# Contractions over 448 rows as pairs of 64-row passes, with the loads and the start rearranged

## Chip, cores, metric

One core of one Trainium2 chip. The metric is the device time of one execution in microseconds (us). Most executions agree within 0.3%. A ratio of two kernels is the mean of one kernel's fast runs over the mean of the other's fast runs of the same rounds on the same chip, so it is not quite the ratio of the medians quoted beside it. The profile's "span" runs from the first to the last instruction; timed runs lie about 2 us above it.

## The reference, cut to what matters

```python
# S = 2048 tokens, D = 448, 16 query heads, 8 KV heads, Dh = 256, window W = 512, F = 1792
xn = layernorm(x)
q  = xn @ wq                                 # 448 -> 4096
p  = softmax(q k^T / 16)                     # over the last 512 keys
s  = (p v) @ wo                              # 4096 -> 448
g  = silu((gelu(xn @ w_gate) * (xn @ w_up)) @ w_down)
out = x + s * g
```

Two stages contract over D = 448: gate/up and Q. A full TensorE pass here contracts over 128 rows, and 448 = 3 x 128 + 64 = 7 x 64.

## The kernel before

A small planner records operations in program order, and puts each on one engine with semaphore waits. Order within an engine is program order, so what is emitted first is issued first. Matmuls write to PSUM, eight banks of 512 columns; a bank is free again when ScalarE or VectorE has read it out (evacuation). The tokens are 4 chunks of 512. Gate/up is 56 units (4 chunks of 14 blocks of 128 columns), and each unit makes a gate and an up tile of 128 x 512. Three 128-row passes and one 64-row remainder make a tile. Remainders of gate (rows 0 to 63) and up (rows 64 to 127) run side by side:

```python
def gu_full(n, b, first, halves=1):          # cut: halves
    for (w, bl, bb) in ((wg, b_wgl[wi], b), (wu, b_wul[wi], b + 1)):
        mms([(bank[bb], w[:, k, cols], xnT[:, k, toks], first and k == 0, (not first) and k == 2, False)
             for k in range(3)], ...)
def gu_rem(n, b, first):
    mms([(bank[b],     wg[0:64, 3, cols],   xnT[0:64, 3, toks],   first, not first, False),
         (bank[b + 1], wu[64:128, 3, cols], xnT[64:128, 3, toks], first, not first, False)], ...)

for sg in range(NSG):                        # a superunit is four units
    n = 4 * sg
    gu_full(n, 0, True); gu_full(n + 1, 2, True)
    ln_more()                                # statistics, normalization, DMA transpose of one more token tile
    gu_rem(n, 0, False);  gu_evac(n, 0)      # evacuation: Gelu on ScalarE, product on VectorE
    gu_rem(n + 1, 2, False); gu_evac(n + 1, 2)
    gu_rem(n + 2, 4, True); gu_rem(n + 3, 6, True)
    gu_full(n + 2, 4, False); gu_evac(n + 2, 4)
    ln_more()
    gu_full(n + 3, 6, False); gu_evac(n + 3, 6)
    if sg == 1:
        for i in range(Hq // 4): load_wq(i)  # 12 DMAs, issued by GpSimd
        for g in range(Hkv): load_v(g)       # 8 more
    if sg == 6: ...                          # K, wo, residual x
    if sg in {5: 0, 8: 1, 11: 2}: down(...)
```

The normalization needs 1/sqrt(var), and that is made by two tiny GpSimd operations:

```python
def ln_stats(t):                             # cut
    K.op("dve",  ... bn_stats, bn_aggr ...)
    K.op("pool", ... ve = var + eps ...)
    K.op("pool", ... rstd = ve ** -0.5 ...)
```

Q is built four heads at a time in the same form. Then for each head: scores (8 matmuls of 512 columns), Exp on ScalarE, value product (16 matmuls of 257 columns), and VectorE divides. `wo` follows once per chunk (128 matmuls of 448 columns).

The softmax here doesn't subtract the row's maximum and nothing guards it: scores larger than these inputs give would overflow.

## Time and profile before

585.99 us median of 3 (585.34 to 586.48), span 583.7 us.

The profile page of the kernel before: the busy tenths of TensorE and its granted clock in 40 equal slices (14.6 us each), and the chain of waits by engine.

```profile
PE   3939999999999999999999999999999999999997
...
PEclk9978999999999999999999999999999999999999
...
PE 92%; POOL 3%; DMA 2%; DVE 1%; ACT 1%; issue 0%; SPq 0%; DVEq 0%
```

TensorE is the limit nearly everywhere. The third slice (29 to 44 us) has a hole, and the clock is below full in the third and fourth slices.

"Busy" hides what a pass costs, because passes overlap: one of 512 columns is recorded as 379 ns long. What tells is the distance between starts (a slot: one pass, or one pair of 64-row passes): 216 ns for 512 columns, 189.5 for 448, 113 for 257, and 216.5 for a pair of 64-row passes (whose two starts are 3 to 4 ns apart). Times their counts:

| stage | slots | ns | us |
|---|---|---|---|
| gate/up | 392 | 216.5 | 84.9 |
| Q | 448 | 216.5 | 97.0 |
| scores | 512 | 216 | 110.6 |
| value product | 1024 | 112.7 | 115.4 |
| wo | 512 | 189.5 | 97.0 |
| down | 224 | 189.5 | 42.4 |
| sum | | | 547.3 |

So 36.4 us of the span are not this work. The largest piece is the hole. The timeline of TensorE in the kernel before (start in us, length, engine, line, operation; in brackets the idle time before it and what ended it):

```profile
31.55 0.81 PE L308 MATMUL bank<-xnT,wg 128*128 128x512 bf16 x3
42.09 1.46 PE L308 MATMUL bank<-xnT,wu 128*128 128x512 bf16 x3 [9.74 <-DVE actT L445]
43.35 1.49 PE L308 MATMUL bank<-xnT,wg 128*128 128x512 bf16 x3
44.63 1.49 PE L308 MATMUL bank<-xnT,wu 128*128 128x512 bf16 x3
```

The timeline of GpSimd in the same stretch:

```profile
26.27 0.57 POOL L353 TENSOR_TENSOR rstd<-ve,nhalf 128x1 f32<-128x1 f32 x1
26.78 7.33 POOL L293 DMA_DIRECT2D wq<-in_A_wq_dram  x12
34.10 5.97 POOL L293 DMA_DIRECT2D va<-in_A_v_cache_dram  x8
40.09 0.24 POOL L351 TENSOR_SCALAR ve<-mv 128x1 f32<-128x1 f32 x1
```

And of VectorE:

```profile
28.52 0.18 DVE L350 BATCH_NORM_AGGREGATE mv<-stats 128x2 f32<-128x6 f32 x1
41.02 0.41 DVE L358 TENSOR_SCALAR xn<-x_65,mv,rstd 128x512 bf16<-128x512 bf16 x1 [12.32 <-POOL rstd L353]
```

Read the three together: GpSimd issues loads for 13.3 us, the small rstd operation stands behind them, VectorE stands behind rstd, the products that would free PSUM stand behind the normalization, and TensorE runs out of PSUM banks. After the hole three 512-column passes take 1.28 us from start to start instead of 0.65: the clock is granted at half until 47.5 us.

The second piece is spread out. The timeline of TensorE, one mixed group of the kernel before:

```profile
140.36 0.81 PE L308 MATMUL bank<-xnT,wu 128*128 128x512 bf16 x3
141.10 0.39 PE L308 MATMUL bank<-xnT,wg 64*128 64x512 bf16 x1
141.11 0.39 PE L308 MATMUL bank<-xnT,wu 64*128 64x512 bf16 x1
141.33 0.38 PE L308 MATMUL bank<-xnT,wg 64*128 64x512 bf16 x1
...
141.76 0.38 PE L308 MATMUL bank<-xnT,wg 64*128 64x512 bf16 x1
141.77 0.38 PE L308 MATMUL bank<-xnT,wu 64*128 64x512 bf16 x1
142.07 0.82 PE L308 MATMUL bank<-xnT,wg 128*128 128x512 bf16 x3
```

From 141.76 to 142.07 is 0.31 us where 0.216 would do, and it is the same on the way in (140.36 to 141.10 is two steps of 0.216 and one of 0.31). A change costs 95 ns, and there are sixty. The Trainium skill, "TensorEngine Tiling (Array Packing)", Key Properties, says that changing the tiling mode drains TensorE. This trace fits that, and gives the price.

Third, where the last down block meets the first scores:

```profile
161.74 1.92 PE L308 MATMUL bank<-qT,kT 128*128 128x512 bf16 x7
164.66 1.95 PE L308 MATMUL bank<-qT,kT 128*128 128x512 bf16 x8 [1.00 <-ACT expT L299]
```

### The profile page before, as it was taken

How to read it: one execution, taken by the hardware profiler on the slowest of the kernel's cores; microseconds unless marked ns; L12 is line 12 of the kernel's file. 1: busy time of each engine (PE TensorE's matmuls, PEld its weight loads, DVE VectorE, ACT ScalarE, POOL GpSimd, SP SyncE). 2: the span in 40 equal slices, each digit the busy share in tenths (PEclk: the TensorE clock that was granted, in tenths of full speed). 3: DMA queues.
4: the chain of work that ended last, by engine and by line, in shares of the span. 5: the costliest groups of instructions: out<-in, count | busy, mean ns of one | idle time of the engine just before them, and what ended most of it. 6: DMA issues, size and time to landing. Idle time of an engine off the chain costs nothing.

```text
span 583.7 us, 8116 instructions
## 1 busy us (share of the span) xinstructions
PE 559.8 (96%) x3260; PEld 300.8 (52%) x3260; DVE 274.3 (47%) x729; ACT 205.1 (35%) x270; POOL 43.1 (7%) x85
## 2 busy tenths in 40 slices
PE   3939999999999999999999999999999999999997
PEld 2313444444455565555565555556556456556653
DVE  3616543434345665513565561265566217557532
ACT  2313232323264455402446441135543203553500
POOL 5382220000000000000000000100000000000000
PEclk9978999999999999999999999999999999999999
DMA  9997599000003311311322230132232113243221
GB/s 255 253 312 168 126 166 161 5 0 2 1 18 55 73 38 36 73 33 31 73 47 46 55 68 21 45 66 43 41 73 47 35 40 53 44 65 60 42 45 33
DMA packets 96565, 41.53 MB, mean 71 GB/s; under 512 B 87840, under 2 KB 92848, under 8 KB 96528
## 3 DMA queue, kind: packets, MB, share of 16 engines
q1 hardware_dynamic: 90864, 24.17, 23.4%
q0 software_dynamic: 4416, 15.70, 10.0%
q10 hardware_dynamic: 1248, 1.15, 0.6%
q8 instruction: 26, 0.43, 0.3%
q14 instruction: 11, 0.09, 0.1%
HBM read 18.71 MB, written 1.84 MB: 35 GB/s over the span
## 4 chain that ended last, share of the span: by engine, by line
PE 92%; POOL 3%; DMA 2%; DVE 1%; ACT 1%; issue 0%; SPq 0%; DVEq 0%
PE bank L308 92%; DMA wu<-in_B_w_up_dram 1%; POOL wq L293 1%; POOL va L293 1%; DMA x_65<-in_A_x_dram 1%; DVE actT L445 0%; POOL rstd L353 0%; DVE stats L349 0%; ACT L299 0%; ACT gl L299 0%; ACT expT L299 0%; POOL wg L293 0%; POOL ve L351 0%; SPq L293 0%; DVE xn L358 0%
## 5 line engine op out<-in xcount | busy, mean ns | idle before, releaser
L299 ACT ACTIVATE expT<-bank 128x1024 bf16<-128x1024 f32 x128 | 124.0, 1021 | 145.9 <-PE bank L308 145.9
L546 DVE TENSOR_SCALAR onorm<-bank,rden 128x256 bf16<-128x256 f32 x256 | 123.8, 484 | 9.3 <-DVE rden L544 0.3
L308 PE MATMUL bank<-va,expT 128*128 128x257 bf16 x1024 | 123.4, 273 | 0.0
L308 PE MATMUL bank<-qT,kT 128*128 128x512 bf16 x512 | 121.1, 379 | 1.1 <-ACT expT L299 1.0
L308 PEld LDWEIGHTS bank<-va,expT 128*128 128x128 bf16 x1024 | 98.4, 98 | 27.2 <-DVE onorm L546 3.0
L308 PE MATMUL bank<-xnT,wq 128*128 128x512 bf16 (+1 forms) x512 | 105.1, 379 | 0.0
L308 PE MATMUL bank<-wo,oT 128*128 128x448 bf16 x512 | 97.5, 352 | 0.0
L308 PEld LDWEIGHTS bank<-qT,kT 128*128 128x128 bf16 x512 | 49.7, 98 | 55.3 <-ACT expT L299 1.9
L522 DVE CAST qT<-bank 128x512 bf16<-128x512 f32 x64 | 42.8, 689 | 68.7 <-PE bank L308 68.7
L308 PEld LDWEIGHTS bank<-wo,oT 128*128 128x128 bf16 x512 | 50.1, 98 | 46.8
L308 PE MATMUL bank<-xnT,wu 128*128 128x512 bf16 (+2 forms) x230 | 61.8, 386 | 10.0 <-DVE actT L445 9.7
L308 PEld LDWEIGHTS bank<-xnT,wq 128*128 128x128 bf16 (+1 forms) x512 | 41.2, 97 | 55.8 <-issue 13.6
L299 ACT ACTIVATE qT<-bank 128x512 bf16<-128x512 f32 x64 | 36.6, 598 | 91.0 <-PE bank L308 91.0
L544 DVE RECIPROCAL rden<-bank 128x1 f32<-128x1 f32 x256 | 40.9, 160 | 58.0 <-PE bank L308 58.0
L308 PE MATMUL bank<-xnT,wg 128*128 128x512 bf16 (+2 forms) x230 | 61.6, 385 | 0.0
L299 ACT ACTIVATE gl<-bank 128x512 bf16<-128x512 f32 x56 | 31.9, 596 | 67.0 <-PE bank L308 67.0
L445 DVE TENSOR_TENSOR actT<-bank,gl 128x512 bf16<-128x512 f32 x56 | 36.9, 687 | 27.7 <-ACT gl L299 21.9
L566 DVE SCALAR_TENSOR_TENSOR tmp<-bank,g_57 128x448 f32<-128x448 f32 x16 | 10.0, 624 | 77.8 <-PE bank L308 77.8
L308 PE MATMUL bank<-wd,actT 128*128 128x448 bf16 x224 | 43.0, 352 | 0.0
L293 POOL DMA_DIRECT2D xr<-in_A_x_dram x16 | 8.6, 540 | 396.4 <-DVE ofin L569 396.4
L308 PEld LDWEIGHTS bank<-xnT,wu 128*128 128x128 bf16 (+1 forms) x230 | 21.7, 100 | 30.6 <-DVE actT L445 10.2
L308 PEld LDWEIGHTS bank<-xnT,wg 128*128 128x128 bf16 (+1 forms) x230 | 20.6, 100 | 32.4 <-issue 13.4
(28 smaller groups left out, 114.8 us busy)
## 6 DMA issues: line engine op xcount, KB each, us to landing
wo<-in_A_wo_dram POOLq DMA_DIRECT2D x4, 896.0 KB, 10.3
wq<-in_A_wq_dram POOLq DMA_DIRECT2D x4, 768.0 KB, 8.1
va<-in_A_v_cache_dram POOLq DMA_DIRECT2D x8, 256.0 KB, 11.8
oT<-onorm SPq DMA_TRANSPOSE x128, 2.5
xr<-in_A_x_dram POOLq DMA_DIRECT2D x16, 112.0 KB, 2.3
out_dram<-ofin SPq DMA_DIRECT2D x16, 112.0 KB, 1.7
wd<-in_B_w_down_dram POOLq DMA_DIRECT2D x1, 1568.0 KB, 12.4
wq<-in_A_wq_dram POOLq DMA_DIRECT2D x8, 128.0 KB, 8.0
```

The lines of the kernel that those rows point to most:

```text
L293: K.op(q, lambda e, o=o, i=i: e.dma_start(o, i), reads, writes, dma=True)
L299: K.op("act", lambda e, o=o, i=i: e.activation(o, i, func, scale=scale), reads, writes)
L308: ins = e.matmul(o, lhsT=l, rhs=r, start=st, stop=sp)
L445: K.op("dve", lambda e: e.tensor_tensor(actT[:, c % 2, f, :], bank[b + 1], gl[:, s, :], ALU.mult), (b_ps[b + 1], b_gl[s]), (b_actT[c % 2][ ...
L522: K.op("dve", lambda e: e.tensor_copy(qT[:, i, h4, 1, :], bank[b + 1]), (b_ps[b + 1],), (b_qT[i][h4][1],))
L544: K.op("dve", lambda e, bb=bb, r=r: e.reciprocal(rden[:, r:r + 1], bank[bb][:, Dh:Dh + 1]), (b_ps[bb],), (b_rden[r],))
L546: K.op("dve", lambda e, bb=bb, r=r, t4=t4: e.tensor_scalar(onorm[:, o, t4, h % 2, :], bank[bb][:, 0:Dh], rden[:, r:r + 1], None, op0=ALU.m ...
L566: K.op("dve", lambda e: e.scalar_tensor_tensor(out=tmp[:, s, :], in0=bank[b][:, 0:D], scalar=0.5, in1=g2[:, t, :], op0=ALU.mult, op1=ALU.m ...
```

## The change

Every contraction over D becomes seven 64-row pairs and nothing else. Weights of one output sit in partitions 0 to 63, those of another in 64 to 127, and the transposed activations are held twice, once in each half. Gate pairs with up. In Q a head pairs with the head four further on, so Q is built for 8 heads at a time. In the same change the loads, the start, the Exp table, the order around the last down block and the tail are rearranged. The core of the diff (cuts marked):

```diff
-        xnT [P, 4, S]; wg, wu [P, 4, F]; wq [P, 4, HD]
+        xnT [P, NK, S]; wgu [P, NK, F]; wq [P, NK, NG, HG // 2, 2, P]     # NK = 7, HG = 8, NG = 2
+        def pair(b, w, x, ks, start, stop, lo=0, hi=QC):
+            return [(bank[b + j][:, lo:hi], w(k)[R * j:R * j + R], x(k)[R * j:R * j + R],
+                     start and k == ks[0], stop and k == ks[-1]) for k in ks for j in range(2)]
   ... normalization writes 7 x 2 x 64 columns, each 64 twice, in place of 512:
+            src = x4[:, t, :].rearrange("p (k r) -> p k r", r=R).unsqueeze(2).broadcast_to([P, NK, 2, R])
   ... loads: the second copies of x's last 64 columns are gone; gate/up weights on the SP queue
   ... (the first up block on ScalarE's), w_down behind x and ahead of every transpose:
+        load_x("sp", 8, 8)
+        dma("sp", wd[:, :, :], B_w_down.rearrange("(f p) d -> p f d", p=P), (), (b_wd,))
   ... start: warm-up matmuls on zeros, half-units (units for 256 of their 512 tokens)
   ... between the transposes of tiles 2 and 3:
+        warm(14, 3)
+        ln_stats(0); ln_stats(1); ln_norm(0); ln_tp_pe(0, ...); warm(2, 3)
+        ln_norm(1); ln_tp_pe(1, [("dve", 4, 0, 4), ("act", 5, 4, NK)]); warm(3, 3)
+        ln_stats(2); ln_stats(3); gu(0, 0)
+        ln_norm(2); ln_tp_pe(2, ...); gu(1, 0); ln_norm(3); ln_tp_pe(3, ...); gu(2, 0)
   ... units: statistics of a tile in an even unit, its normalization in the odd unit after
+        for n in range(NQC * NF):
+            gu(n); gu_evac(n); ...
-            if sg == 1:                     # wq, V
+            if n == 27:                     # wq, V, K: behind the last rstd (unit 24)
+        DOWN_AT = {NF + 1: 0, 2 * NF + 3: 1, 3 * NF + 1: 2}
+        act(tmp[:, 1, 0:1], nhalf[:, :], ACT.Exp, ...)          # loads Exp's table ahead of Q
   ... first scores before the last down block; last output tile in two halves of 224 columns
```

## The prediction

> **What bounds it now.** TensorE. The chain of waits is 92% matmuls; the page gives PE 96% busy. Reading the distance between matmul starts in the timeline: a 512-column pass starts every 216 ns, a 257-column one every 113 ns, a 448-column one every 189.5 ns, and a pair of 64-row passes (starts 4 ns apart) every 216.5 ns. Multiplied by their counts (gate/up 392 slots, Q 448, scores 512, value 1024, output 512, down 224) this is about 547 us that the PE cannot avoid. Span 583.7 less 547 leaves 37 us:
> - start: first gate matmul at 11.3 us, then about 1 us at half clock and a 0.4 us wait for weights;
> - one hole at 32.2 to 42.1 us (9.9 us). Timeline: GpSimd issues 12 wq and 8 va loads from 26.8 to 40.1 us, and the tiny ops that make rstd stand behind them; VectorE, in order, waits 12.3 us for rstd, so it does not drain PSUM. The clock record shows half clock to 47.5 us, which costs another 2.7 us;
> - about 60 changes between 128-row and 64-row passes: the start distance is 308 to 312 ns there instead of 216, so 94 ns each, 5.7 us. The Trainium skill, "TensorEngine Tiling (Array Packing)", Key Properties, says that changing the tiling mode drains TensorE; this trace agrees and prices it;
> - 1.6 us at 163 us, where the first Exp waits for Tanh and a 1.28 us table load;
> - 3.9 us after the last matmul start.
>
> **What the change does.** The number of PE slots does not fall: two outputs cost 6 full passes plus one pair before, 7 pairs after, 7 slots either way. More weight loads (14 for 8), but the two halves load together in about 95 ns, inside the 216 ns slot. So the pairing itself gains only changes of mode: gate/up keeps them only around the three down blocks, Q has 8 groups in place of 16 pair blocks, about 22 left. Gain 3.5 us.
>
> The larger gain is in what moves with it. wq, va go to unit 27, after the last rstd (unit 25): the 9.9 us hole and its 2.7 us of half clock go. Exp's table is loaded before Q, and the first scores come before the last down block: 1.6 us go. The last output block is halved: 0.5 us.
>
> Start: the duplicate x loads go (the first norm waits 2.1 us for them before), and warm-up matmuls precede. But normalization writes 896 columns instead of 512 (0.41 us before; 0.65 to 1.0, estimated by size), each tile has 7 transposes instead of 4, and tiles 2 and 3 come late: I estimate the first half-units at 8.5 us and gap-free running from 13.6 us, 2.3 us of work being done by then.
>
> xnT's DMA transposes get 7/4 as long and queue behind wd (6 us to landing before); tile 7 is needed at about 34 us, I expect it by 30. VectorE in chunk 0 carries at most 2.5 us per 3.0 us.
>
> **Sum.** 13.6 + (547.3 - 2.3) + 2.1 changes of mode + 3.4 tail = 564 us span; the timed runs lie 2 us above: 566 us, range 560 to 573. Over 2% faster: 0.95; within: 0.04; slower: 0.01.
>
> **Right if:** no PE wait above 1 us after 15 us; pairs in Q and gate/up stay at 216 to 217 ns; the 308 ns steps fall to about 22; clock full from about 15 us; DVE waits for rstd under 2 us.
>
> **Wrong if:** long rows of pairs run slower than four do (10 ns per slot is 8 us); the weights, now to 64 partitions per transfer, land after 10 us; a longer start cools the clock; xnT transposes arrive late at chunk 1; the broadcast norm is much over 1 us.

## The result, and the profile after

566.75 us median of 4 (565.94 to 567.22) against 586.23; ratio 0.9669 (95% interval 0.9652 to 0.9686). It is 3.3% faster. Span 565.4 us.

The page of the changed kernel, the same lines (slices of 14.1 us):

```profile
PE   7989999999999999999999999999999999999997
...
PEclk9999999999999999999999999999999999999999
...
PE 93%; DVE 3%; issue 1%; DMA 1%; POOL 1%; ACT 0%; DVEq 0%; ACTq 0%
```

The large hole and the half clock are gone. A small hole is left, in the third slice. From the waits view, who waited for rstd in the kernel before (in all, times, longest, us):

```profile
DVE xn L358 <- POOL rstd L353: 26.0, 13, 12.3
```

and in the changed kernel:

```profile
DVE xn L356 <- POOL rstd L350: 5.8, 15, 0.5
```

The timeline of TensorE in the changed kernel, one Q group of 8 heads between a value product and the next scores:

```profile
179.79 2.23 PE L308 MATMUL bank<-va,expT 128*128 128x257 bf16 x18
181.95 12.26 PE L308 MATMUL bank<-xnT,wq 64*128 64x512 bf16 x112
194.37 2.97 PE L308 MATMUL bank<-qT,kT 128*128 128x512 bf16 x13 [0.16 <-issue]
```

In this long row of pairs the two starts lie 3 to 4 ns apart and the next pair follows 216 ns after the last, as in the short rows of before. Going in, the step is 207 ns after a 257-column pass instead of 113, and the next is 227 instead of 216. Coming out, the records are 535 ns apart, because the record of the first score pass is missing in this profile (15 of the 16 are there, 13 of them in this window). In profiles of the later variants x_best and a_no_warm, whose Q stage is the same, it is there: 308 ns after the last start, and the next follows 227 ns later. So a change costs about 106 ns in these long rows too, each way. After the start there are 21 changes in place of 60: six around the three down blocks, seven into Q (the first Q group follows gate/up directly) and eight out of it.

The start of the changed kernel, from the timeline of TensorE:

```profile
8.96 1.06 PE L308 MATMUL bank<-xnT,wgu 64*128 64x256 bf16 x14 [0.29 <-DVE mv L347]
10.72 0.56 PE L372 MATMUL bank<-ident,xn 128*128 128x128 bf16 x7 [0.70 <-DVE xn L356]
11.21 0.94 PE L308 MATMUL bank<-xnT,wgu 64*128 64x256 bf16 x14
12.28 0.56 PE L372 MATMUL bank<-ident,xn 128*128 128x128 bf16 x7
12.78 1.48 PE L308 MATMUL bank<-xnT,wgu 64*128 64x256 bf16 x24
```

From 12.78 us it runs without a gap, with two half-units (1.5 us) already done. The hole that is left, same view:

```profile
29.66 2.97 PE L308 MATMUL bank<-xnT,wgu 64*128 64x512 bf16 x26
34.71 3.20 PE L308 MATMUL bank<-xnT,wgu 64*128 64x512 bf16 x28 [2.09 <-DMA xnT<-xn]
```

and the SP queue ahead of it (here length is the time over which the group is issued):

```profile
10.78 5.20 SPq L296 DMA_DIRECT2D wd<-in_B_w_down_dram  x1
20.03 17.02 SPq L299 DMA_TRANSPOSE xnT<-xn  x6
```

Unit 14 is the first of chunk 1 and needs tiles 4 to 7. The semaphore records say: w_down lands at 30.7 us, the transpose issued at 20.03 (tile 4) at 31.5, that of tile 7, issued at 31.2, at 34.6.

What stands around the 547.3 us of passes, term by term. Each is read from the distances between starts, the clock record and the ends of the span:

| us | before | after |
|---|---|---|
| first gate matmul, less work done by gap-free running | 11.3 | 12.8 - 1.5 = 11.3 |
| half clock and weights at the start | 1.5 | 0 |
| hole near 32 us | 9.9 | 2.25 |
| half clock after it | 2.7 | 0 |
| changes of mode | 60 x 0.106 = 6.4 | 21 x 0.106 = 2.2 |
| scores around the last down block (wait for its product on VectorE, then for Exp) | 1.4 | 0.3 |
| from the last matmul's start | 4.2 | 3.2 |
| sum with 547.3 | 584.7 (span 583.7) | 566.6 (span 565.4) |

Most of what the sums lie above the spans is the 0.8 us by which 547.3 is high. The count of slots is the same in both columns: 448 rows cost 7 slots for two outputs, either as 6 full passes and one pair, or as 7 pairs.

### The profile page after: what moved, and what is told of

Same layout as the page of the kernel before. It is cut to its first block, busy times and chain, and to the rows that moved or that the text cites. A ratio compares the mean times of both kernels' runs of the same rounds, so it can differ in the third digit from the quotient of the medians.

```text
span 565.4 us, 9758 instructions
## 1 busy us (share of the span) xinstructions
PE 553.6 (98%) x4037; PEld 310.6 (55%) x4073; DVE 284.3 (50%) x736; ACT 209.3 (37%) x272; POOL 34.5 (6%) x70
## 4 chain that ended last, share of the span: by engine, by line
PE 93%; DVE 3%; issue 1%; DMA 1%; POOL 1%; ACT 0%; DVEq 0%; ACTq 0%
PE bank L308 93%; DVE actT L426 1%; DVE stats L346 1%; POOL rstd L350 1%; DVE xn L356 1%; DMA xnT<-xn 1%; DMA x_65<-in_A_x_dram 0%; PE bank L372 0%; POOL ve L348 0%; DVE mv L347 0%; DVE xnT L382 0%; DVE g_57 L437 0%; ACT gl L302 0%; ACT tmp L302 0%; PE bank L390 0%
## 5 line engine op out<-in xcount | busy, mean ns | idle before, releaser
L308 PE MATMUL bank<-qT,kT 128*128 128x512 bf16 x476 | 115.9, 379 | 2.9 <-issue 1.3
L308 PE MATMUL bank<-xnT,wq 64*128 64x512 bf16 x896 | 98.1, 376 | 0.0
L308 PE MATMUL bank<-wo,oT 128*128 128x448 bf16 (+1 forms) x544 | 97.6, 341 | 0.0
L308 PE MATMUL bank<-xnT,wgu 64*128 64x512 bf16 (+1 forms) x826 | 86.0, 366 | 2.4 <-DMA xnT<-xn 2.1
L308 PEld LDWEIGHTS bank<-wo,oT 128*128 128x128 bf16 x544 | 53.1, 98 | 44.0
L308 PEld LDWEIGHTS bank<-xnT,wq 64*128 64x128 bf16 x896 | 43.0, 94 | 52.9 <-issue 1.5
L308 PEld LDWEIGHTS bank<-xnT,wgu 64*128 64x128 bf16 x826 | 39.8, 94 | 47.9 <-DVE actT L426 2.6
L563 DVE SCALAR_TENSOR_TENSOR tmp<-bank,g_57 128x448 f32<-128x448 f32 (+1 forms) x17 | 10.2, 597 | 82.5 <-PE bank L308 82.5
L308 PEld LDWEIGHTS bank<-wd,actT 128*128 128x128 bf16 x224 | 21.7, 98 | 21.2 <-issue 1.3
L437 DVE SCALAR_TENSOR_TENSOR g_57<-tmp,bank 128x448 bf16<-128x448 f32 x16 | 9.9, 622 | 33.8 <-ACT tmp L302 33.8
## 6 DMA issues: line engine op xcount, KB each, us to landing
wgu<-in_B_w_gate_dram SPq DMA_DIRECT2D x2, 560.0 KB, 11.5
```

Of the source, the lines that this page charges most:

```text
L308: ins = e.matmul(o, lhsT=l, rhs=r, start=st, stop=sp)
L437: K.op("dve", lambda e, t=t, b=b, s=s: e.scalar_tensor_tensor(out=g2[:, t, :], in0=tmp[:, s, :], scalar=1.0, in1=bank[b][:, 0:D], op0=ALU. ...
L563: K.op("dve", lambda e: e.scalar_tensor_tensor(out=tmp[:, s, c0:c1], in0=bank[b][:, c0:c1], scalar=0.5, in1=g2[:, t, c0:c1], op0=ALU.mult, ...
```

## Experiments

The theory: of 18.3 us of span, some 10.4 come from where the loads are issued (12.6 less the new hole of 2.25), 4.1 from fewer changes of mode, the rest from the start, the Exp table and the tail. The rival: the pairing carries the gain. All kernels below gave correct results.

### The loads alone, in the kernel before

```diff
-            if sg == 1:
-                ... load_wq, load_v
             if sg == 6:
+                ... load_wq, load_v
```

> The kernel before, with one edit: the 12 wq and 8 va loads are issued after superunit 6 (where K is loaded), not after superunit 1. No pairing. Theory (the hole of 9.9 us at 32 us and its 2.7 us of half clock come of GpSimd issuing those loads ahead of the rstd ops): 12 to 13 us faster, 573 to 574 us, so two thirds of the whole change's gain without any of the pairing. Rival (the pairing itself carries the gain, and the loads only move a stall to another place): under 6 us faster.

Measured: 574.6 us median (574.44 to 575.41) against 586.3, ratio 0.9803. That is 11.7 us without any pairing, about 60% of the whole gain. GpSimd makes rstd at 26.9, 29.8, 33.8 and 36.8 us, with no issues between, and the clock is full from 14 us on. The gain is just under the 12 to 13 expected. (The spans of the two profiles differ by 10.7 us.) In the place of the hole stand three small waits of TensorE for VectorE, of about 0.6 us each by the distances between starts (the waits view of this kernel: in all, times, longest):

```profile
PEld bank L308 <- DVE actT L445: 2.8, 3, 0.9
```

### And the Exp table

```diff
+        act(tmp[:, 1, 0:1], nhalf[:, :], ACT.Exp, (b_nhalf,), (b_tmp[1],))
         def q_full(...)
```

> As the last, and one dummy Exp before Q, so that its table is loaded early. Theory (the wait at 163 us is Tanh's evacuation plus the 1.28 us table load): 1.3 us faster than the last; the hole before the second scores shrinks from 1.2 us to under 0.3 us. Rival (the wait is for the Exp itself, 1.02 us each): no gain.

Measured: 573.8 us (573.53 to 575.15), ratio 0.9794 (0.9777 to 0.9811) against 0.9803 (0.9788 to 0.9818): the times alone do not tell them apart. The traces show the wait, and what goes with it. With the loads late only:

```profile
151.29 1.91 PE L308 MATMUL bank<-qT,kT 128*128 128x512 bf16 x7
154.21 1.52 PE L308 MATMUL bank<-qT,kT 128*128 128x512 bf16 x6 [1.01 <-ACT expT L299]
```

With the table loaded early as well:

```profile
150.85 4.07 PE L308 MATMUL bank<-qT,kT 128*128 128x512 bf16 x15
154.75 0.50 PE L308 MATMUL bank<-va,expT 128*128 128x257 bf16 x3
```

The wait of 1.2 us is gone, but two waits for Exp of about 0.2 us each take its place: from the last down pass to the first value pass it is 4.31 us against 5.11, so 0.8 us are gained there, not 1.3. In this profile a 1.1 us wait for gate/up weights at 18.9 us, which the other did not have, takes that back, and an earlier first gate matmul (10.9 against 11.8 us) gives about as much again. Weights land up to about 1.2 us apart between profiles of one kernel (the first gate weights at 8.7 us in the changed kernel, at 9.9 us in its control), so small gains at the start or near it need a trace beside the times.

### Control, and Q in groups of four

The changed kernel once more, on the chip of the next three:

> Control: the changed kernel once more, on the same chip as the next three, so that differences under 1% can be read against it. Both theories: 566 to 567 us, with one hole of 2.4 us near 32 us where gate/up unit 14 waits for the transpose of tile 7.

Measured: 567.08 us (566.72 to 568.95), ratio 0.9679; the hole is there, 2.0 us.

```diff
-    HG = 8
+    HG = 4
```

> The changed kernel with Q in groups of 4 heads instead of 8, everything else the same: 16 Q blocks instead of 8, so 16 more changes between 64-row and 128-row passes. Theory (the pairing gains only the changes of mode, some 95 ns each in the trace, 103 ns on leaving Q): 16 x 0.097 = 1.6 us slower than the control, with 308 to 319 ns at every block edge and no other new gap. Rival (the group of 8 pays by something else, such as fewer waits for PSUM or for the Q copies): the difference is well off 1.6 us, or appears as idle time at other places.

Measured: 569.6 us (567.72 to 570.29), ratio 0.9710; by the ratios 1.8 us over the control, with overlapping intervals. The trace is sharper: the distance from one chunk's first Q group to the next chunk's is 105.8 us against 105.26 in the control, 0.54 us for two more Q groups, or 2.1 us over four chunks. Changes of mode explain 0.21 us a group (106 in, 106 out), 1.7 us in all. The edges are those of the larger groups: 535 ns out, with one record missing, in all 16. So the price of a change holds, and some 0.06 us a group are left; in the trace a value-product step of 155 to 157 ns in place of 112 comes with each added group, and what it waits for was not followed up.

### Pairs not side by side

```diff
-                     start and k == ks[0], stop and k == ks[-1]) for k in ks for j in range(2)]
+                     start and k == ks[0], stop and k == ks[-1]) for j in range(2) for k in ks]
```

> The changed kernel with the passes of a pair not side by side: all 7 lower halves of a unit, then all 7 upper ones; same instructions, same count, same result. Theory (a pair costs one slot only because its two passes are neighbours in program order and run in the two halves at once): each unit takes 14 slots instead of 7, so 840 x 0.216 = 181 us slower, about 748 us. Rival (TensorE overlaps lower and upper halves whatever their order): under 620 us.

Measured, in one look: 576.61 us, span 574.8, state unknown (one run). My theory of the pair was wrong here: it lost 9.4 us of span, not 181. The timeline of TensorE, the Q group that corresponds to the one shown above:

```profile
186.72 12.92 PE L308 MATMUL bank<-xnT,wq 64*128 64x512 bf16 x112
199.80 2.54 PE L308 MATMUL bank<-qT,kT 128*128 128x512 bf16 x11 [0.16 <-issue]
```

The group takes 13.08 us from its start to the next stage's, against 12.42 above. Within it, two passes start in every 216 ns, 19 and 197 ns apart, although seven of one half stand behind one another in program order; only the first three and the last three or four passes of a row go singly, one per 216 ns. Two passes of the same half never overlapped where they could be seen alone, so a pass of the other half must have started ahead of passes that stand before it in the program. The records do not name the half, but they do mark the last pass of each unit, by the semaphore that it raises. In the changed kernel it is the 14th, 28th, 42nd to start in this row, as in the program; here it is the 17th, 31st, 45th, up to the last unit. So three passes of the next unit started ahead of it, and the upper half runs three passes behind the lower. What adjacency buys is only the ragged ends: 0.66 us a row of pairs (one record is missing at the end of the row in both), 7.3 us over the 11 long rows. The other 2 us lie in the first row, whose start ran at half clock until 17.5 us in this run; the hole at unit 14 is gone there, since the later start hides it. The Trainium skill, "TensorE: Matmul & The Clock Gate", Part 3, The mechanism ("What overlaps and what doesn't"), calls matmuls strictly first-in first-out in start and end; the starts in this run do not agree. (The ends are modelled in these profiles.)

### The small hole: w_down behind the transposes

```diff
-        dma("sp", wd[:, :, :], ...)          # ahead of all transposes
+            if n == 9:                       # behind tile 7's transpose
+                dma("sp", wd[:, :, :], ...)
```

> The changed kernel with the load of w_down issued behind the transpose of tile 7 (unit 9) instead of ahead of all transposes. Theory (the 2.4 us hole at 32 us comes of the xnT transposes standing in the queue behind w_down, which lands at 30.7 us): tile 7 lands before 31 us, the hole is gone, 2.4 us faster than the control; w_down lands by about 35 us, in time for the first down block near 36 us. Rival (the transposes are slow by their own length or by the SP engine's issue): the hole stays at over 1 us, and the gain is under 1 us.

Measured: 569.59 us (568.07 to 571.68), ratio 0.9726, which is 2.5 us slower than the control. The hole for the transpose is gone (tile 7 lands at 32.5 us, in time, though later than I expected), and a new one stands a little further on, because w_down now lands at 38.4 us. From the timeline of TensorE:

```profile
33.64 2.12 PE L308 MATMUL bank<-xnT,wgu 64*128 64x512 bf16 x18
38.55 1.71 PE L308 MATMUL bank<-wd,actT 128*128 128x448 bf16 x6 [2.79 <-DMA wd<-in_B_w_down_dram]
```

In this profile the clock record also shows half clock from 39.3 to 42.7 us, 1.7 us more. The cause of the hole was right; the cure moved the wait.

With the start reordered as well (statistics of tile 2 before the first normalization, those of tile 3 after the second, tile 1's copy all on ScalarE):

> As the last, and the start reordered on VectorE: statistics of tile 2 before the first normalization, and of tile 3 right after the second, the PSUM copy of tile 1 all on ScalarE. Theory (the start is bound by the chain of normalizations on VectorE, which puts tiles 2 and 3 late): gap-free running begins near 11.5 us instead of 13.6, another 2 us faster, 562 us in all. Rival (the first weights, landing at 8.4 to 8.7 us, or a clock that is half until about 9 us bind the start): no gain over the kernel with w_down late alone.

Measured: 569.79 us (568.71 to 571.75), ratio 0.9722, no gain. Gap-free running began at 12.69 us, not 11.5: tile 2's transpose stood on TensorE behind half-unit 0, which waits for tile 1's copy, and VectorE's next normalization stood behind tile 2's copy. And whatever the start gains is lost at the same landing of w_down (39.4 us). The hole there is 4.1 us, yet the clock record stays at full after it, while the 2.9 us hole of the run before was followed by half clock: these runs do not show from what length a hole costs clock.

```diff
-        DOWN_AT = {NF + 1: 0, ...}
+        DOWN_AT = {NF + 5: 0, ...}           # with w_down late, as above
```

> The changed kernel with w_down's load behind tile 7's transpose, as before, and the first down block after unit 19 in place of 15, so that it begins near 41 us instead of 35. Theory (both holes, 2.4 us for the transpose in the changed kernel and 2.9 us for w_down in the first variant, are waits for the same DMA engines, and w_down lands at 38.4 us): no PE gap over 0.5 us between 15 us and the end, 2 to 2.5 us faster than the changed kernel, ratio to before about 0.964. Rival: the wait moves on to tiles 8 to 11 or elsewhere, no gain.

Measured: 565.38 us (564.7 to 567.06), ratio 0.9647 (0.9632 to 0.9662) against the control's 0.9679 (0.9664 to 0.9694): about 1.9 us by the ratios, just under the 2 to 2.5 expected (the two ran on different chips, each against the kernel before on its own). From 13.7 us to the Q stage no step between starts is over 0.31 us, the edges included. The start of the profiled run was late (first weights waited for, 2.1 us).

### The start, once the hole is gone

```diff
+        ln_stats(2)                          # ahead of ln_norm(0)
         ...
-        ln_tp_pe(1, [("dve", 4, 0, 4), ("act", 5, 4, NK)])
+        ln_tp_pe(1, [("act", 5, 0, NK)])
         warm(3, 3)
+        ln_stats(3); ln_norm(2); ln_norm(3)
+        ln_tp_pe(2, [("dve", 7, 0, NK)])
+        gu(0, 0)
+        ln_tp_pe(3, [("dve", 4, 0, 4), ("act", 6, 4, NK)])
+        gu(1, 0); gu(2, 0)
```

on top of the last kernel.

> As x_wd_d19, with the four normalizations in a row on VectorE and the transposes of tiles 2 and 3 not behind half-units of gate/up in the queue of TensorE. Theory (the reordered start of before failed because the transposes and PSUM copies of tiles 2 and 3 still stood behind half-unit 0, which waits for tile 1's copy): gap-free running begins at 9.5 to 10.5 us instead of 13.1 with 1.5 us of work done, so 1 to 2 us faster than x_wd_d19. Rival (weights, landing between 8.4 and 9.7 us, and the half clock until 9 to 13 us bind): no gain beyond 0.5 us.

Measured: 564.38 us (562.91 to 564.99), ratio 0.9623 (0.9610 to 0.9636). It beats both kernels: about 2.5 us under the changed one and 22 us under the kernel before. From the timeline of TensorE:

```profile
10.14 0.94 PE L308 MATMUL bank<-xnT,wgu 64*128 64x256 bf16 x14 [0.31 <-DMA wgu<-in_B_w_gate_dram]
...
11.51 20.61 PE L308 MATMUL bank<-xnT,wgu 64*128 64x256 bf16 x224
32.71 0.61 PE L308 MATMUL bank<-xnT,wgu 64*128 64x512 bf16 x4 [0.59 <-issue]
```

Half-unit 0 now waits for its weights (0.3 us), gap-free running begins at 11.5 us (9.5 to 10.5 was expected) with 0.8 us done, about 0.5 us of work ahead of the changed kernel's profile. A step of 0.97 us (0.75 more than plain) is left at 31.75 us, where tile 7 lands at 32.6 by the semaphore records (the view names no releaser). Over the last kernel it is 1.4 us by the ratios (the intervals overlap slightly), in the range expected; how much of that is the run-to-run landing of weights is open.

### The warm-up

All three `warm(...)` calls taken out of the changed kernel:

> The changed kernel without the 19 warm-up matmuls. Theory (they bring the full clock to about 9 us[...]): full clock from 13 to 17 us, 1 to 2 us slower. Rival (the first real work is short of data anyway, so the clock there costs nothing): within 0.5 us.

Measured: 567.09 us (566.77 to 567.29), ratio 0.9673 against 0.9679 and 0.9669: no difference. From the timeline of TensorE:

```profile
9.99 1.67 PE L308 MATMUL bank<-xnT,wgu 64*128 64x256 bf16 x14 [2.24 <-DMA wgu<-in_B_w_gate_dram]
...
14.70 22.66 PE L308 MATMUL bank<-xnT,wgu 64*128 64x256 bf16 x234
```

The clock is full only from 14.4 us and gap-free running begins at 14.7 us, later than with the warm-up, just as the theory had it. But the hole at unit 14 shrinks to one step of 0.42 us, since tile 7 lands at 34.5 us in any case, and the first row of pairs ends at 37.4 us, against 37.5 and 37.6 in the two profiles with the warm-up. The rival's number was right for another reason than it gave: up to unit 14 the start is not what binds; the landing of tile 7 is.

### The loads early, in the changed kernel

```diff
-            if n == 27:
+            if n == 7:
```

> The changed kernel with its wq and va loads issued after unit 7 instead of 27, which is where the kernel before had them. Theory (a blocked GpSimd holds up rstd, then VectorE, then PSUM): a hole comes back between 25 and 45 us, with tile 7's normalization some 7 us late, and the time rises by 6 to 14 us, with half clock after the hole. Rival (paired running is immune, since it has other PSUM order): under 2 us slower.

Measured: 611.42 us (609.91 to 614.21), ratio 1.0434. The edit was not what its description says: the block also holds the K transposes, so these moved ahead of tile 7's as well. Its size is therefore not that of the loads alone. Its trace, of a fast run, still shows what the loads do to the transposes. The SP queue, then TensorE:

```profile
20.29 35.81 SPq L299 DMA_TRANSPOSE xnT<-xn  x3
56.14 20.05 SPq L299 DMA_TRANSPOSE kT<-in_A_k_cache_dram  x8
...
79.54 4.80 PE L308 MATMUL bank<-xnT,wgu 64*128 64x512 bf16 x24 [46.85 <-DMA xnT<-xn]
```

Tiles 5 and 6, issued at 28.7 and 31.2 us and so ahead of every K transpose, land at 65.2 and 68.5 us by the semaphore records; the last of wq lands at 60.8, the last of va at 67.9. The run was redone with K left where it was:

> The run before with wq and va early also moved the K transposes early, against its description; here K stays at unit 27 and only wq and va go to unit 7. First theory (GpSimd's issue time holds up rstd, VectorE and PSUM, as in the kernel before): PE's hole ends with VectorE, lasts 3 to 8 us, the time rises by 6 to 14 us. Second theory (here the transposes of x's tiles meet 5.7 MB of loads on the same DMA engines, 20 us at some 280 GB/s): the hole ends with the landing of a transpose, tile 5, 6 or 7 at 45 us or later, lasts 12 us or more, and the time rises by 15 to 40 us.

Measured: 599.94 us median of 4 (595.25 to 997.87), ratio of the fast runs 1.0207 (1.0172 to 1.0241), about 31 us slower than the changed kernel. One run, the profiled one, is slow: 997.87 us at a granted clock of 0.56. So its trace serves only for what ended the wait, not for the size. From its timeline of TensorE:

```profile
45.67 4.09 PE L308 MATMUL bank<-xnT,wgu 64*128 64x512 bf16 x20
64.42 3.17 PE L308 MATMUL bank<-xnT,wgu 64*128 64x512 bf16 x14 [14.67 <-DMA xnT<-xn]
```

The wait ends with the landing of a transpose, as the second theory has it: tile 7's, at 64.3 us. Tile 6's, issued at 35.8 us, lands at 60.1, after the last of wq at 56.2. In the kernel before the same placement of the loads delayed rstd; in this one it delays the landing of the transposes, though these stand in another queue, by that trace and by the fast one of the run before, and it costs more. No fast run of this kernel has a trace, so the split of its 31 us is open.

## Why the prediction was right

It said 566 us, 560 to 573, and 566.75 was measured. Point by point:

- "The number of PE slots does not fall": shown. Pairs step at 216 ns in rows of 112 to 280 passes as they did in rows of eight, and the loads alone, without pairs, gave 11.7 of 19 us.
- "the 9.9 us hole and its 2.7 us of half clock go": shown by the kernel before with late loads; 11.7 us by the medians, 10.7 by the two profiled spans, less than 12.6 because VectorE's queue makes three small waits (1.8 us together) in its place.
- "about 22 left. Gain 3.5 us" (changes of mode): 21 left. The count was right and the price low: 106 ns each, since the step after a change is longer too, so 39 x 0.106 = 4.1 us. Groups of four heads cost 2.1 us by the trace and 1.8 by the ratios, where 1.6 was expected. No run took the pairing alone.
- Exp and the order around the last down block: 1.1 us (1.4 to 0.3) in place of 1.6; a wait of 0.3 us for VectorE's product is left at 156.2 us.
- Start: first half-unit at 8.96 us (said 8.5); 12.78 with 1.5 us done is what 13.6 with 2.3 done was to be. The normalization took 0.74 us (said 0.65 to 1.0). What was wrong is the worth of the warm-up, which the prediction listed under the start without a figure: taking it out changed nothing.
- Tail: 0.9 us gained (4.16 to 3.23) in place of 0.5.
- Wrong: "tile 7 is needed at about 34 us, I expect it by 30". It was needed at 32.4 and landed at 34.6, for a hole of 2.25 us, and the test "no PE wait above 1 us after 15 us" failed. The first figure is an error of sum: 13.6 + 14 x 1.516 - 2.3 is 32.5. The second left out that the first transpose, behind w_down in the queue, would land only after it (w_down at 30.7 us, tile 4 at 31.5); the other three then came in 3.2 us. It was on the list of what could go wrong. That the total still came within 1.4 us of the predicted span, 564, is in part luck: the passes, about 0.8 us less than counted, and the tail hid some of the hole.

## What to carry to other kernels

Before paying for a new layout, multiply slots by start distances and list what is left over; here the layout left the slots as they were, and more than half of the gain was one block of load issues standing in an engine's queue ahead of a 0.6 us operation. A hole that a DMA's landing ends absorbs whatever is gained or lost before it: the start was worth nothing until the landing was moved, and then moving one load only put the wait on the load that had been moved. Try an improvement again after the wait behind it is gone.

## What the Trainium skill lacked or had wrong

- "TensorEngine Tiling (Array Packing)", Key Properties: says that a change of tiling mode drains TensorE, without a price. Here it is 106 ns each way between 128-row and 64-row passes, after short rows and long: 95 in the step itself (311 ns in place of 216, 207 in place of 112) and 11 in the step after it (227 in place of 216).
- "TensorE: Matmul & The Clock Gate", Part 3, The mechanism: strict first-in first-out for matmuls, in start and end. With seven passes of one half ahead of seven of the other, two passes still began every 216 ns, only three or four at each end of a row went alone, and the last pass of a unit, 14th in the program, was the 17th to start. Neighbouring order was worth 0.66 us a row.
- The same page, Part 1, names grants of half and full, 13/16 under three busy cores, and a clock seen stuck at 1/4. One run here, on one core, was granted 0.555 for 928 us.
- "DMA: Bandwidth & Descriptors": I found no figure for a DMA transpose that stands behind plain loads in its queue. Here 2.9 us from issue to landing when quiet, 11.4 us behind w_down, and next to 5.8 MB of loads from another queue 36 to 37 us (tiles 5 and 6 in the fast run with the loads and K early) and 24 us (tile 6 in the slow run).
